# Second MoE of a fused attention and two-MoE kernel: operands in halves, result additions on GpSimd

## The chip, the cores and the metric

One core of one Trainium2 chip. The metric is the device time in microseconds of one execution, the median of three runs. TensorE (PE in the profile) multiplies, VectorE (DVE), ScalarE (ACT) and GpSimd (POOL) work elementwise, and SyncE (SP) issues the transfers. Each engine works through its own instructions in the order in which they are written; semaphores make it wait for others.

## The reference

An attention over 4 batches, 8 heads, 576 positions and 64 columns (half the heads with a local mask, half with a strided one) gives 2304 tokens of 512 columns. Two MoE blocks follow:

```python
gate = 1.0 / (1.0 + np.exp(-(x @ w_gate)));  x = gate * (x @ w_val) @ w_out
h = x @ w_in                                   # 512 -> 2048
g = np.maximum(h, 0.0) + np.log1p(np.exp(-np.abs(h)))
return g @ w_out                               # 2048 -> 512
```

The change lies in the second block (the last three lines).

## The kernel before, in words

Every number is kept as a high and a low part (`xh`, `xl`; `gh`, `gl`), and every product is three matmuls: high by high, high by low, low by high (`mm3`, lines 72 to 74). An operand is made of a float32 tile in two steps: `high` copies it on ScalarE into the rounded part, and `low` subtracts that part from the tile on VectorE or GpSimd (`make`, line 516, with `minus`, line 330). A tile here is 128 partitions by 2 rows of 512 columns, the two rows being the two chunks (`c` or `k`) of the 256 columns of the hidden layer in one group.

The second block (`moe2`, lines 409 to 771) handles the tokens in two halves of 1024 (the last 256 tokens go along with the second half in `short_up` and `short_unit`). Each half goes through 8 groups, so `nn` runs from 0 to 15; `m` counts pairs of groups. Both multiplications are done by a scheme with seven products in place of eight on two-by-two blocks: sums of blocks are formed first, the products are made, and sums of products give the result.

A group `nn` on the way up has seven products, `mul(0)` to `mul(6)`, each six matmuls (`product`). Behind each, `fill(k)` puts some units of the way down (`downs`, numbers in `counts`). A unit is six matmuls into one of three PSUM tiles `ps_y`, and then one VectorE instruction (line 469, or 467 for the first) adds them to a sum in SBUF and so frees the PSUM tile. Between products and units stand hooks: `at(n, k, ph, fn)` registers work for group `n` behind `mul(k)` (`ph` 0) or behind `fill(k)` (`ph` 1). This order, written out by hand, is the order on every engine.

A group gives a 2 by 2 block of activations: `bi` and `bj` with two rows each. `chain` is three ScalarE instructions (absolute value, exponential, logarithm), `finish` one VectorE instruction that adds the positive part. Row 0 of `bi` is done behind `mul(3)`, row 1 of `bj` behind `mul(4)` (`finish(s5)`, line 747), row 0 of `bj` behind `mul(5)` (`add_to(u2)`, chain, and `finish(u2)`, line 752), and row 1 of `bi` behind `mul(6)` (chain, and a `finish` that stands at the head of the next group's first hooks). `snap`, at `mul(0)` of the next group, copies a product into the PSUM tile `ps_b` (line 720) on which `mul(2)` goes on adding.

From the four blocks of a pair of groups (`n1` odd, `n2` after it) seven operands are made: B11, T1, B22, T3, T2, T4, B21. Their tiles `gh` and `gl` come from a pool with three of each: a new operand gets a tile whose units are over. GpSimd makes the sums of blocks in place (`sub(POOL, ...)`): `b12` becomes `b22 - b12`, from which T3 is made, and `b11` becomes `b22 - b11`, from which T2 is made. In the last pair of each half (`m` 3) four plain operands `gj0`, `gi0`, `gj1`, `gi1` replace the seven, and their units add to the results themselves. Shortly before, seven additions of 128x1024 make the results of the sums kept so far (lines 607 to 614, `nl` being 6 and 14). Their tiles `a` and `p6` are called `raw` in the trace, the others `acc`.

The places that are named in the sections below, by the order of the units: the units of T1 stand in `fill(6)` of `n1` and `fill(0)` of `n2`, those of B22 in `fill(1)` and `fill(2)` of `n2`, those of T2 in `fill(5)` and `fill(6)`; in group 7 the first unit of `gj0` stands in `fill(3)`, in group 15 as well. Group 15 has two or three units in each fill. Behind group 15 the last ten units follow, two by two, with hooks between (lines 762 to 770).

Of the kernel before, what the change touches and what calls it, by code (L numbers as in the profile page):

```python
# [40 lines left out]
GC = 2  # L41
# [7 lines left out]
def tile_sparse_attention_moe_moe2(  # L49
# [282 lines left out]
    def high(op, src):  # L332
        nc.scalar.activation(out=op[0], in_=src, func=AF.Copy)  # L333

    def low(op, src, eng):
        minus(eng, op[1], src, op[0].bitcast(F32))
# [58 lines left out]
    def moe2(pools, buf):  # L395
# [55 lines left out]
            load_down(0, home)  # L451


        def unit(key, e, op, y, init, last=False, store=None):
            def go():
                w = at_w[key][0]
                ps = bank(pools, "y", "ps_y")
                o = slice(e * P, (e + 1) * P)
                for c in range(GC):
                    mm3(  # L460
                        ps, (w[:, c, 0, o], w[:, c, 1, o]), tuple(x[:, c, :] for x in op()),
                        c == 0, c == GC - 1,
                    )
                if last:
                    free(key)
                if init:
                    nc.vector.tensor_copy(y, ps)
                else:
                    nc.vector.tensor_tensor(out=y, in0=ps, in1=y, op=ALU.add)  # L469
                if store is not None:  # L470
                    nc.sync.dma_start(out=store, in_=y)

            return go
# [32 lines left out]
        def at(n, k, ph, fn):  # L506
            hooks.setdefault((n, k, ph), []).append(fn)

        def new_op():
            return tuple(  # L510
                pools["g"].tile([P, GC, TB], F32R, tag=x, name=x) for x in ("gh", "gl")
            )
# [3 lines left out]
        def make(op, src, eng, first, second):  # L516
            def begin():
                op.extend(new_op())
                high(op, src)

            at(*first, begin)
            at(*second, lambda: low(op, src, eng))

        def sub(eng, out, a, b):
            return lambda: minus(eng, out, a, b)

        def plus(eng, out, a):
            return lambda: eng.tensor_tensor(out=out, in0=out, in1=a, op=ALU.add)
# [4 lines left out]
        for half in range(2):  # L533
            ac = accs[half]
            for m in range(NM):
                n0 = half * NG2 + 2 * m
                n1, n2, n3 = n0 + 1, n0 + 2, n0 + 3
                b11, b12 = even[m % 2]
                b21, b22 = odd
                key = lambda name: (half, m, name)  # L540
                ops = {x: [] for x in ("B11", "T1", "B21", "B22", "T2", "T3", "T4")}
                get = lambda x, ops=ops: (lambda: ops[x])
                queues.setdefault(n1, [])
                queues.setdefault(n2, [])
                queues.setdefault(n3, [])
                if m == NM - 1:
                    gj0, gi0, gj1, gi1 = [], [], [], []
                    make(gj0, b12, DVE, (n0, 6, 1), (n1, 0, 0))
                    make(gi0, b11, DVE, (n1, 2, 0), (n1, 2, 1))
                    make(gj1, b22, DVE, (n1, 6, 1), (n2, 0, 0))  # L550
                    make(gi1, b21, DVE, (n2, 0, 1), (n2, 1, 0))
                    for nn, par, gj, gi in ((n1, 0, gj0, gi0), (n2, 1, gj1, gi1)):
                        names = (("A11", "A21"), ("A12", "A22"))[par]
                        for t, op, cs in (
                            (2 * half + 1, gj, ("C12", "C22")), (2 * half, gi, ("C11", "C21"))
                        ):
                            for d, c in enumerate(cs):
                                for e in range(2):
                                    d0 = (2 * d + e) * P
                                    t0 = blocks[t][0]  # L560
                                    queues[nn].append(unit(
                                        key(names[d]), e, lambda op=op: op, ac[c][:, e, :], False,
                                        op is gi and e == 1 and (half == 0 or False),
                                        out[d0:d0 + P, t0:t0 + TB] if par else None,
                                    ))
                        if half == 1:
                            for d in range(2):
                                queues[nn].append(short_unit(
                                    key(names[d]), 2 * m + par, d, (2 * m + par) % 2, True
                                ))  # L570
                    continue
                make(ops["B11"], b11, DVE, (n1, 0, 1), (n1, 1, 0))
                at(n1, 1, 1, sub(POOL, b11, b12, b11))
                make(ops["T1"], b11, POOL, (n1, 3, 0), (n1, 3, 1))
                make(ops["B22"], b22, DVE, (n1, 6, 1), (n2, 0, 0))
                at(n1, 6, 1, sub(POOL, b12, b22, b12))
                at(n2, 0, 1, sub(POOL, b11, b22, b11))
                make(ops["T3"], b12, DVE, (n2, 1, 0), (n2, 1, 1))
                make(ops["T2"], b11, DVE, (n2, 2, 0), (n2, 2, 1))
                at(n2, 2, 1, sub(POOL, b11, b21, b11))  # L580
                make(ops["T4"], b11, POOL, (n2, 4, 0), (n2, 4, 1))
                make(ops["B21"], b21, POOL, (n2, 5, 1), (n2, 6, 0))

                def both(nn, name, x, last=True):
                    for e in range(2):
                        queues[nn].append(unit(
                            key(name), e, get(x), ac[target[name]][:, e, :], m == 0,
                            last and e == 1,
                        ))

                alone = half == 0
                both(n1, "A11", "B11", alone)
                if half == 1:
                    for d, name in enumerate(("A11", "A21")):
                        queues[n1].append(short_unit(key(name), 2 * m, d, 0, True))
                both(n1, "S1", "T1")
                for name, x in (("S4", "B22"), ("S3", "T3"), ("S2", "T2")):
                    both(n2, name, x)
                both(n2, "A22", "T4", alone)
                if half == 1:  # L600
                    queues[n2].append(short_unit(key("A22"), 2 * m + 1, 1, 1, True))
                both(n2, "A12", "B21", alone)
                if half == 1:
                    queues[n2].append(short_unit(key("A12"), 2 * m + 1, 0, 1, True))


            nl = half * NG2 + NG2 - 2
            at(nl, 1, 1, plus(POOL, ac["C11"], ac["a"]))
            at(nl, 3, 1, plus(POOL, ac["C12"], ac["C22"]))
            at(nl, 6, 1, plus(DVE, ac["a"], ac["p6"]))  # L610
            at(nl + 1, 0, 0, plus(DVE, ac["C12"], ac["a"]))
            at(nl + 1, 0, 1, plus(POOL, ac["a"], ac["p7"]))
            at(nl + 1, 1, 0, plus(POOL, ac["C22"], ac["a"]))
            at(nl + 1, 1, 1, plus(POOL, ac["C21"], ac["a"]))
# [37 lines left out]
        def chain(src, dst):  # L652
            nc.scalar.activation(out=dst, in_=src, func=AF.Abs)
            nc.scalar.activation(out=dst, in_=dst, func=AF.Exp, scale=-1.0)
            nc.scalar.activation(out=dst, in_=dst, func=AF.Ln, bias=1.0)

        def finish(src, dst):
            nc.vector.scalar_tensor_tensor(
                out=dst, in0=src, scalar=0.0, in1=dst, op0=ALU.max, op1=ALU.add
            )  # L660
# [31 lines left out]
        for nn in range(N):  # L692
# [13 lines left out]
            def mul(k, ps, a, b, first, stop, then_do=None):  # L706
                product(ps, a, x[b], first, stop)
                if then_do:
                    then_do()
                if not last and (half == 0 or a not in OPS[:3]):  # L710
                    fetch(goes, then, a)
                run_hooks(k, 0)
# [24 lines left out]
            if half == 1 and not last:  # L737
# [5 lines left out]
            add_to(s5, Bk, s5)  # L743
            chain(s5, bj[:, 1, :])
            fill(4)
            mul(5, D, "S4", "B22", False, True)
            finish(s5, bj[:, 1, :])
            add_to(u2, D, u2)
            chain(u2, bj[:, 0, :])
            fill(5)  # L750
            mul(6, Bk, "A22", "T4", False, True)
            finish(u2, bj[:, 0, :])
            chain(Bk, bi[:, 1, :])
            hooks.setdefault((nn + 1, 0, 0), []).insert(
                0, lambda Bk=Bk, d=bi[:, 1, :]: finish(Bk, d)
            )
# [680 lines left out]
```

## Time and profile before

| | us |
|---|---|
| runs (3), median and extremes | 901.35 (899.46 to 901.43) |
| the profiled execution | 902.33 |
| its span (first to last instruction) | 900.5 |
| PE busy in the span | 874.0 (97%) |
| DVE, ACT, POOL busy | 608.5, 413.6, 453.6 |
| mean granted TensorE clock | 0.988 |

The span is the time between the first and the last instruction of the profiled execution. An engine is busy while it executes; instructions of TensorE overlap, and a matmul of 512 columns lasts longer than the distance between two of them. "Idle before" counts from the end of the instruction before it on the same engine, and the name behind it is what ended the wait.

### The profile page before, as it was taken

How to read it: one execution, taken by the hardware profiler on the slowest of the kernel's cores; microseconds unless marked ns; L12 is line 12 of the kernel's file. 1: busy time of each engine (PE TensorE's matmuls, PEld its weight loads, DVE VectorE, ACT ScalarE, POOL GpSimd, SP SyncE). 2: the span in 40 equal slices, each digit the busy share in tenths (PEclk: the TensorE clock that was granted, in tenths of full speed). 3: DMA queues.
4: the chain of work that ended last, by engine and by line, in shares of the span. 5: the costliest groups of instructions: out<-in, count | busy, mean ns of one | idle time of the engine just before them, and what ended most of it. 6: DMA issues, size and time to landing. Idle time of an engine off the chain costs nothing.

```text
span 900.5 us, 15316 instructions
## 1 busy us (share of the span) xinstructions
PE 874.0 (97%) x6022; PEld 729.4 (81%) x6022; DVE 608.5 (68%) x893; ACT 413.6 (46%) x663; POOL 453.6 (50%) x353
## 2 busy tenths in 40 slices
PE   7699999999999999999999999999999999999997
PEld 5578878888888888888888887888778888888786
DVE  6596776278878887788884545565786464657755
ACT  2366544333333232333243556667557565555541
POOL 5373421047796786687677425655642243343510
PEclk9699999999999999999999999999999999999999
DMA  9686450034764575566552435655455664545403
GB/s 272 175 240 166 121 157 1 1 117 138 253 229 175 187 256 168 182 230 209 195 210 94 141 98 190 199 199 191 153 199 186 204 192 153 176 148 171 137 1 116
DMA packets 59974, 149.33 MB, mean 166 GB/s; under 512 B 6048, under 2 KB 6560, under 8 KB 59904
## 3 DMA queue, kind: packets, MB, share of 16 engines
q1 hardware_dynamic: 59616, 147.75, 50.9%
q8 instruction: 47, 0.77, 0.4%
q10 hardware_dynamic: 288, 0.62, 0.2%
q14 instruction: 23, 0.19, 0.1%
HBM read 112.17 MB, written 36.18 MB: 165 GB/s over the span
## 4 chain that ended last, share of the span: by engine, by line
PE 66%; DVE 7%; ACT 3%; POOL 2%; issue 2%; DVEq 0%; POOLq 0%; ACTq 0%
PE ps_y L73 9%; PE ps_y L72 9%; PE ps_y L74 9%; PE ps_v L74 4%; PE ps_v L72 4%; PE ps_v L73 4%; PE ps_g L72 4%; PE ps_g L73 4%; PE ps_g L74 4%; PE ps_h L74 3%; PE ps_h L73 3%; PE ps_h L72 3%; PE ps_b L73 2%; PE ps_b L72 2%; PE ps_b L74 2%
## 5 line engine op out<-in xcount | busy, mean ns | idle before, releaser
L330 POOL TENSOR_TENSOR b<-b,b 128x1024 f32<-128x1024 f32 x24 | 60.3, 2524 | 110.3 <-DVE gl L330 60.9
L241 ACT ACTIVATE gh<-ps_v 128x512 fp32r<-128x512 f32 (+1 forms) x60 | 33.2, 554 | 128.8 <-DVE ps_v L284 128.8
L304 DVE TENSOR_TENSOR acc<-ps_y,acc 128x512 f32<-128x512 f32 (+1 forms) x100 | 61.9, 632 | 39.0 <-PE ps_y L74 38.3
L469 DVE TENSOR_TENSOR acc<-ps_y,acc 128x512 f32<-128x512 f32 x72 | 48.7, 687 | 43.4 <-PE ps_y L74 43.3
L189 POOL TENSOR_TENSOR a<-f,e 128x512 f32<-128x512 f32 x32 | 41.4, 1294 | 58.3 <-DVE e L139 57.9
L242 DVE TENSOR_TENSOR gl<-ps_v,gh 128x512 fp32r<-128x512 f32 (+1 forms) x60 | 38.3, 638 | 40.0 <-ACT gh L241 40.0
L330 POOL TENSOR_TENSOR gl<-b,gh 128x1024 fp32r<-128x1024 f32 x18 | 43.3, 2406 | 37.6 <-ACT gh L333 37.6
L284 DVE TENSOR_TENSOR ps_v<-ps_v,sg 128x512 f32<-128x512 f32 (+1 forms) x60 | 38.5, 642 | 28.0 <-PE ps_v L74 26.6
L333 ACT ACTIVATE gh<-b 128x1024 fp32r<-128x1024 f32 x50 | 52.5, 1050 | 10.3 <-POOL b L330 9.7
L73 PE MATMUL ps_y<-gl,w12h 128*128 128x512 f32 (+1 forms) x148 | 55.3, 374 | 1.0 <-DVE gl L330 1.0
L72 PE MATMUL ps_y<-gh,w12h 128*128 128x512 f32 (+1 forms) x148 | 55.9, 378 | 0.5 <-ACT gh L333 0.4
L72 PE MATMUL ps_y<-gh,w02h 128*128 128x512 f32 (+1 forms) x144 | 54.8, 381 | 0.8 <-ACT acc L302 0.5
L73 PE MATMUL ps_y<-gl,w02h 128*128 128x512 f32 (+1 forms) x144 | 54.0, 375 | 0.4 <-DVE gl L242 0.4
L330 DVE TENSOR_TENSOR gl<-b,gh 128x1024 fp32r<-128x1024 f32 x32 | 47.6, 1486 | 8.9 <-ACT gh L333 8.9
L126 DVE SCALAR_TENSOR_TENSOR f<-raw,ps_x 128x512 uint32<-128x512 uint32 x68 | 46.8, 688 | 9.8 <-POOL w11l L153 2.1
L74 PE MATMUL ps_y<-gh,w02l 128*128 128x512 f32 (+1 forms) x140 | 52.3, 373 | 0.4 <-POOL w02l L153 0.4
L74 PE MATMUL ps_y<-gh,w12l 128*128 128x512 f32 (+1 forms) x140 | 52.2, 373 | 0.2 <-POOL w12l L153 0.2
L177 POOL TENSOR_TENSOR pair<-a,pair 128x512 fp32r<-128x512 f32 x32 | 41.4, 1295 | 18.9 <-ACT pair L176 18.2
L139 DVE SCALAR_TENSOR_TENSOR e<-raw,ps_x 128x512 f32<-128x512 uint32 x68 | 46.7, 687 | 2.3
L132 DVE TENSOR_SCALAR ps_x<-f 128x512 uint32<-128x512 uint32 x68 | 46.8, 688 | 1.1
L122 DVE TENSOR_SCALAR ps_x<-raw 128x512 uint32<-128x512 uint32 x68 | 46.5, 684 | 0.0
L72 PE MATMUL ps_g<-xh,w00h 128*128 128x512 f32 (+1 forms) x120 | 45.3, 378 | 0.0
(341 smaller groups left out, 2768.8 us busy)
## 6 DMA issues: line engine op xcount, KB each, us to landing
raw<-in_w_dram SPq DMA_DIRECT2D x68, 512.0 KB, 3.9
in_s<-pair SPq DMA_DIRECT2D x32, 512.0 KB, 2.8
xh<-in_s SPq DMA_DIRECT2D x64, 256.0 KB, 3.3
out_s<-pair SPq DMA_DIRECT2D x28, 512.0 KB, 2.7
xl<-in_s SPq DMA_DIRECT2D x56, 256.0 KB, 3.5
out_dram<-acc SPq DMA_DIRECT2D x16, 256.0 KB, 2.0
w10h<-out_s SPq DMA_DIRECT2D x6, 512.0 KB, 5.9
w10l<-out_s SPq DMA_DIRECT2D x6, 512.0 KB, 4.1
```

What stands on the lines that cost most here:

```text
L72: nc.tensor.matmul(ps, lhsT=lh, rhs=rh, start=first, stop=False, **kw)
L73: nc.tensor.matmul(ps, lhsT=lh, rhs=rl, start=False, stop=False, **kw)
L74: nc.tensor.matmul(ps, lhsT=ll, rhs=rh, start=False, stop=last, **kw)
L122: nc.vector.tensor_scalar(out=part, in0=high, scalar1=3, scalar2=0x3FFFFFFF, op0=ALU.logical_shift_left, op1=ALU.bitwise_and,)
L126: nc.vector.scalar_tensor_tensor(out=f, in0=high, scalar=0xC0000000, in1=part, op0=ALU.bitwise_and, op1=ALU.bitwise_or,)
L132: nc.vector.tensor_scalar(out=e, in0=f, scalar1=0xFF800000, scalar2=None, op0=ALU.bitwise_and)
L139: nc.vector.scalar_tensor_tensor(out=e.bitcast(F32), in0=low, scalar=2.0 ** -52, in1=x.bitcast(F32), op0=ALU.mult, op1=ALU.mult,)
L177: nc.gpsimd.tensor_tensor(out=l, in0=src, in1=h.bitcast(F32), op=ALU.subtract)
L304: nc.vector.tensor_tensor(out=y, in0=ps[:, 0:n], in1=y, op=ALU.add)
L330: eng.tensor_tensor(out=out, in0=a, in1=b, op=ALU.subtract)
L333: nc.scalar.activation(out=op[0], in_=src, func=AF.Copy)
L469: nc.vector.tensor_tensor(out=y, in0=ps, in1=y, op=ALU.add)
```

## The change

The operands that are made last in a group (B22 of each pair, and `gj0`, `gj1`, `gi1` of the last pair of each half) are made row by row, each row 512 columns, the row that is done first ahead of the other (`make_late`). A unit takes its two chunks in the order `order`: chunk 1 first, except for units of `gi`. The two GpSimd sums that read `b22` (for T3 and T2) are cut into rows as well. `finish(s5)` and `finish(u2)` are written ahead of the transfer and the hooks of their product, and a hook of phase 0.5 stands behind the last chain of a group. Two of the seven result additions of each half go from VectorE to GpSimd.

```diff
-        def unit(key, e, op, y, init, last=False, store=None):
+        def unit(key, e, op, y, init, last=False, store=None, order=(1, 0)):
...
-                for c in range(GC):
+                for i, c in enumerate(order):
                     mm3(
                         ps, (w[:, c, 0, o], w[:, c, 1, o]), tuple(x[:, c, :] for x in op()),
-                        c == 0, c == GC - 1,
+                        i == 0, i == GC - 1,
                     )
...
+        def make_late(op, src, nn, k, times):
+            row = lambda k: tuple(x[:, k, :] for x in op)
+
+            def begin():
+                op.extend(new_op())
+                high(row(k), src[:, k, :])
+
+            other = 1 - k
+            for when, fn in zip(times, (
+                begin, lambda: low(row(k), src[:, k, :], DVE),
+                lambda: high(row(other), src[:, other, :]),
+                lambda: low(row(other), src[:, other, :], DVE),
+            )):
+                at(nn + when[0] // 7, when[0] % 7, when[1], fn)
+
+        LATE_J = (1, ((5, 0), (5, 1), (6, 0), (6, 0.5)))
+        LATE_I = (0, ((5, 1), (6, 0.5), (7, 0), (7, 1)))
...
-                    make(gj0, b12, DVE, (n0, 6, 1), (n1, 0, 0))
+                    make_late(gj0, b12, n0, *LATE_J)
                     make(gi0, b11, DVE, (n1, 2, 0), (n1, 2, 1))
-                    make(gj1, b22, DVE, (n1, 6, 1), (n2, 0, 0))
-                    make(gi1, b21, DVE, (n2, 0, 1), (n2, 1, 0))
+                    make_late(gj1, b22, n1, *LATE_J)
+                    make_late(gi1, b21, n1, *LATE_I)
...
+                                        (0, 1) if op is gi else (1, 0),
...
-                make(ops["B22"], b22, DVE, (n1, 6, 1), (n2, 0, 0))
-                at(n1, 6, 1, sub(POOL, b12, b22, b12))
-                at(n2, 0, 1, sub(POOL, b11, b22, b11))
+                make_late(ops["B22"], b22, n1, *LATE_J)
+                for k, when in ((1, (n1, 5, 1)), (0, (n1, 6, 1))):
+                    at(*when, sub(POOL, b12[:, k, :], b22[:, k, :], b12[:, k, :]))
+                for k, when in ((1, (n1, 6, 1)), (0, (n2, 0, 1))):
+                    at(*when, sub(POOL, b11[:, k, :], b22[:, k, :], b11[:, k, :]))
...
-            at(nl, 6, 1, plus(DVE, ac["a"], ac["p6"]))
-            at(nl + 1, 0, 0, plus(DVE, ac["C12"], ac["a"]))
+            at(nl, 6, 1, plus(POOL, ac["a"], ac["p6"]))
+            at(nl + 1, 0, 0, plus(POOL, ac["C12"], ac["a"]))
...
-            mul(5, D, "S4", "B22", False, True)
-            finish(s5, bj[:, 1, :])
+            mul(5, D, "S4", "B22", False, True, lambda d=bj[:, 1, :]: finish(s5, d))
             add_to(u2, D, u2)
             chain(u2, bj[:, 0, :])
             fill(5)
-            mul(6, Bk, "A22", "T4", False, True)
-            finish(u2, bj[:, 0, :])
+            mul(6, Bk, "A22", "T4", False, True, lambda d=bj[:, 0, :]: finish(u2, d))
             chain(Bk, bi[:, 1, :])
+            run_hooks(6, 0.5)
```

## Rows read from the trace of the kernel before

**Rows 1.** Windows: us, busy of PE, PEld, DVE, ACT, POOL (x instructions), PEclk, DMA, GB/s.

```profile
512.30:901.00 388.70, 376.34 (x1828) 315.50 (x1826) 235.91 (x298) 222.97 (x337) 153.75 (x66) 0.99 0.50 161
635.50:639.30 3.80, 3.80 (x11) 2.93 (x11) 3.80 (x4) 0.00 (x0) 1.67 (x1) 0.55 0.00 1
863.20:875.40 12.20, 12.20 (x55) 10.10 (x55) 7.72 (x12) 3.79 (x6) 0.00 (x0) 1.00 0.01 1
```

**Rows 2.** Timeline of PE, matmuls that waited: start, us, instruction, [idle before <-releaser].

```profile
548.95 0.50 PE L73 MATMUL ps_y<-gl,w10l 128*128 128x512 f32 x1 [0.16 <-POOL gl L330]
...
554.86 0.50 PE L72 MATMUL ps_y<-gh,w12h 128*128 128x512 f32 x1 [0.40 <-ACT gh L333]
...
556.38 0.50 PE L73 MATMUL ps_y<-gl,w12h 128*128 128x512 f32 x1 [1.02 <-DVE gl L330]
...
634.98 0.50 PE L73 MATMUL ps_y<-gl,w10h 128*128 128x512 f32 x1 [2.08 <-DVE gl L330]
...
657.22 0.50 PE L72 MATMUL ps_b<-w01h,xl 128*128 128x512 f32 x1 [0.15 <-ACT ps_b L720]
...
661.01 0.50 PE L72 MATMUL ps_y<-gh,w10h 128*128 128x512 f32 x1 [0.78 <-DVE acc L469]
...
776.70 0.50 PE L73 MATMUL ps_y<-gl,w01l 128*128 128x512 f32 x1 [0.26 <-DVE gl L330]
...
853.50 0.47 PE L72 MATMUL ps_y<-gh,w01l 128*128 128x512 f32 x1 [1.67 <-issue]
...
886.22 0.50 PE L72 MATMUL ps_y<-gh,w02l 128*128 128x512 f32 x1 [0.72 <-DVE acc L469]
...
889.41 0.50 PE L72 MATMUL ps_y<-gh,w02h 128*128 128x512 f32 x1 [0.15 <-DVE acc L469]
```

**Rows 3.** Instructions writing ps_y after 512 us: ns min/median/max, first and last start.

```profile
L73 PE MATMUL ps_y<-gl,w10h x24: 389/390/537, 543.2 to 662.0; 128*128 128x512 f32 x24
```

**Rows 4.** Lines L330, L308, L687, then groups of ACT: lengths in ns.

```profile
L330 DVE TENSOR_TENSOR gl<-b,gh x32: 1207/1218/3072, 537.3 to 884.3; 128x1024 fp32r<-128x1024 f32 x32
...
L330 DVE TENSOR_TENSOR xh<-sg,xh x4: 679/682/693, 704.3 to 852.1; 128x512 fp32r<-128x512 f32 x4
...
L308 POOL TENSOR_TENSOR xl<-acc,xh x14: 737/1292/1632, 471.5 to 545.8; 128x512 fp32r<-128x512 f32 x10, 128x256 fp32r<-128x256 f32 x4
...
L687 ACT ACTIVATE xh<-sg x4: 614/624/633, 703.6 to 849.4; 128x512 fp32r<-128x512 f32 x4
...
L333 ACT ACTIVATE gh<-b 128x1024 fp32r<-128x1024 f32 x50 | 52.5, 1050 | 10.3 <-POOL b L330 9.7 <-DVE b L658 0.5
```

**Rows 5.** Timeline of POOL and DVE around 845 us.

```profile
845.24 2.41 POOL L330 TENSOR_TENSOR gl<-b,gh 128x1024 fp32r<-128x1024 f32 x1 [4.21 <-ACT gh L333]
...
845.80 2.94 DVE L528 TENSOR_TENSOR raw<-raw 128x1024 f32<-128x1024 f32 x1
...
852.12 0.68 DVE L330 TENSOR_TENSOR xh<-sg,xh 128x512 fp32r<-128x512 f32 x1
```

**Rows 6.** Timeline of DVE and ACT, groups 1 to 2.

```profile
552.07 0.69 DVE L658 SCALAR_TENSOR_TENSOR b<-raw,b 128x512 f32<-128x512 f32 x1 [1.43 <-ACT b L655]
...
551.95 0.58 ACT L653 ACTIVATE b<-ps_b 128x512 f32<-128x512 f32 x1
...
554.71 0.58 ACT L720 ACTIVATE ps_b<-ps_h 128x512 f32<-128x512 f32 x1
```

**Rows 7.** Timeline of DVE and ACT, groups 5 to 7.

```profile
632.04 2.88 DVE L330 TENSOR_TENSOR gl<-b,gh 128x1024 fp32r<-128x1024 f32 x1 [0.26 <-ACT gh L333]
...
648.07 2.30 DVE L658 SCALAR_TENSOR_TENSOR b<-raw,b 128x512 f32<-128x512 f32 x1 [0.56 <-ACT b L655]
...
654.40 3.08 DVE L528 TENSOR_TENSOR raw<-raw 128x1024 f32<-128x1024 f32 x1
...
656.59 0.58 ACT L720 ACTIVATE ps_b<-ps_h 128x512 f32<-128x512 f32 x1
```

**Rows 8.** Timeline of DVE behind the last group.

```profile
884.34 1.23 DVE L330 TENSOR_TENSOR gl<-b,gh 128x1024 fp32r<-128x1024 f32 x1 [3.37 <-ACT gh L333]
```

## The prediction

> **What bounds the kernel now.** The busy shares by window come first: in the second MoE TensorE is busy 376.3 of 388.7 us [rows 1], so only the gaps between matmuls can be won; the matmuls themselves stay the same. The timeline of PE then shows where it waited [rows 2]. To price a wait I need the even pace: 55 matmuls in 12.20 us without a gap [rows 1], or 0.23 us from start to start. A matmul lasts 0.39 us [rows 3], so it overlaps the next by 0.16; one that waited lasts 0.50 [rows 2], 0.11 more. A wait thus costs its idle time plus 0.16 plus 0.11, or idle plus 0.27.
>
> By place [rows 2]: (a) 548.95, the low part of T1, 0.43. (b) 554.86 and 556.38, operand B22 of group 2, 0.67 and 1.29. (c) 634.98, B22 of group 6, 2.35; right behind it the granted clock averages 0.55 for 3.8 us [rows 1], half speed most of that time, after TensorE had been idle 2.08 us. That costs 0.45 x 3.8 = 1.7, so (c) is 4.05. (d) 657.22, the snapshot in group 7, 0.42. (e) 661.01, a unit waiting for VectorE to free its tile, 1.05. (g) 776.70, B22 again, 0.53; group 14 has a second one alike. (i) 853.50 in group 15, 1.94: its releaser reads "issue", but the unit needs a tile that VectorE frees late. (j) 886.22 and 889.41 behind the last group, 0.99 and 0.42. Without (a), which the change doesn't touch, 1.96 + 4.05 + 0.42 + 1.05 + 1.06 + 1.94 + 1.41 = **11.9 us** can be won.
>
> Why they are late is told by the lengths. A low part of 128x1024 on VectorE takes 1.22 us, but 3.07 at worst; 128x512 takes 0.68 [rows 4]. The cause is seen around 845 us: GpSimd runs 845.24 to 847.65, VectorE starts at 845.80 and ends at 848.74, 1.09 us after GpSimd [rows 5]. A VectorE instruction with both inputs in SBUF stands until GpSimd's is over.
>
> **The halves.** Twelve operands are cut: three B22, `gj0`, `gj1` and `gi1` in each half of the tokens. Each costs two ScalarE halves of 0.62 for one of 1.05 and two VectorE halves of 0.68 for one of 1.22 [rows 4]: 0.2 and 0.14 more, which lie beside TensorE's work. Twelve GpSimd sums become 24 of 1.29 [rows 4] for 12 of 2.41; GpSimd is busy 154 of 389 us [rows 1], so what counts is that one half holds VectorE for 1.29 at most. No transfer is added, and SP's queue keeps its order; `finish` ahead of a transfer's issue is on another engine. The early half's ScalarE part falls into the time in which VectorE does `add_to(u2)`, so the next chain isn't put off.
>
> The late half starts after `finish(u2)`, ahead of the last chain: 0.62 on ScalarE and 0.68 on VectorE, plus at most 1.29 of standing, 2.6 us together. In group 1 `finish(u2)` ends at 552.76 [rows 6], so the late half is there by 555.4, and only the fifth matmul of the unit needs it, 0.9 us into a unit that is due at 554.5. (b) goes as a wait for the operand.
>
> But a new wait stands behind it. The last chain now starts at 552.76 + 0.62 = 553.4 in place of 551.95; from its start to that of the snapshot it was 2.76 us, 1.05 of them the whole high part [rows 6, 4], which leaves 1.8 (the two overlap a little), so the snapshot runs 555.2 to 555.8, and `mul(2)` is due around 555.7. I leave 0.5 of (b): **1.5 won**. Queued behind the late half on VectorE are the addition of `fill(6)` and `finish(Bk)`; three PSUM tiles give that addition 2.7 us.
>
> (c): the low part starts at 632.04 [rows 7], after a chain of 1.9 and a high part of 1.05, so ScalarE was free for the late half at 629.1; by 631.7 it is done, before the unit wants it at 632.9. **4.05 won**, clock included.
>
> (g): group 12 and 14 have more units between, and the snapshot's slack is over 3 us there; **1.1 won**.
>
> (d) and (e): in group 6 the chain is bound by the other engines. `finish(s5)` takes 2.30 at 648.07, held by GpSimd's low part of T4, and the snapshot begins at 656.59 [rows 7]. With 4.05 us gone TensorE is that much ahead, and the others only in part: GpSimd's addition into C11 now meets the low part of T3, which stands for it, and T2, T4 and both chains follow. I estimate 1.0 us more of lateness against TensorE, plus 0.4 for the late half's wait for `finish(u2)`, less 0.43 for a half in place of a whole high part: (d) grows from 0.42 to 1.4. (e) goes, as the 3.08 us addition [rows 7] leaves VectorE. **0.1 won**.
>
> **The additions.** Four leave VectorE, two in each half of the tokens; they took 3.08 and 2.94 [rows 7, 5], and about 1.2 each for the other two, 8.4 together. On GpSimd they are four of 2.41. Undisturbed, one takes 2.41 there against 1.22 [rows 5, 4], so GpSimd has up to 4 x 1.2 = 4.8 us more to do than VectorE would at its best; at the two places that matter VectorE took more than GpSimd does. The Trainium skill speaks against such a move (GPSIMD Engine Reference, 3.1 Elementwise: elementwise work stays on VectorE as a rule, a large add being 1.96 times as long on GpSimd). The trace agrees on the ratio, 2.41 to 1.22, but not at these two places, 2.41 to 3.08 and 2.94; by the rule alone the sum would be 4.8 us smaller, by the rows it is as below. Queued behind the moved ones on GpSimd are the three additions that were there. In group 7 the chain of five starts around 655 and `C12` is ready after two, near 660; its first unit ends near 661.
>
> (i): here three things stand. The pool has three tiles of each kind; the early operand `gj0` now takes the one that B21 took, so B21's high part must wait for the last S2 unit. VectorE's addition of 845.80 [rows 5] needs that unit's eviction of 0.69, so the unit ends near 845.0; B21's high part, 1.05, now starts there in place of 844.1, and GpSimd's low part of 2.41 runs from 846.1 to 848.5. `gj0`'s late half behind it on VectorE stands until then and ends at 849.1. Then the moved addition starts on GpSimd as soon as the last S2 unit is added, at 849.7, holds the port to 852.1, and the short operand's low part (852.12 to 852.80 before [rows 5]) stands to 852.7. The eviction behind it comes at 853.3, as late as now. **0.2 won** of 1.94.
>
> (j): the last high part of `gi1` waits for the short chain; with halves its low part takes 0.68 at 884.0 in place of 1.23 from 884.34 [rows 8]. (886.22) goes, 0.4 is left one unit later. **1.0 won**.
>
> Sum: 1.5 + 4.05 + 1.1 + 0.1 + 0.2 + 1.0 = 7.95. The profiled execution took 902.33, 0.98 above the median of 901.35; 902.33 - 7.95 = 894.4, and against the median **893.4**.
>
> **The rivals.** *All goes* (0.17): the new waits at (b), (d), (i) and (j) stay hidden, 901.35 - 11.9 = 889.4. For it: my new waits hang on tenths. Against: GpSimd's hold is seen in every row that is late.
>
> *GpSimd's sums are late* (0.08): VectorE's first addition into `C12` stands for GpSimd, and every eviction with it. Price: GpSimd's 4.8 us more in full, 893.4 + 4.8 = 898.2. It decides once GpSimd's second sum ends after the first unit of `gj0`, a margin of about 1 us in group 7 and 7 in group 15. (It is the case of the Trainium skill's rule above.)
>
> *The snapshot takes over* (0.11): the last chain starts 1.3 us later (0.69 of `finish(u2)` and 0.62), and 1.6 more where GpSimd holds `finish(u2)` as it held the one at 648.07 (2.30 for 0.69 [rows 7]). Against the slack from the snapshot's end to `mul(2)`, read along the timeline of ACT and PE (0.4, 2.4, 1.4 us in groups 2, 4, 6; none in 7; 1.9 in 8; over 3 later) 2.9 us leaves 2.5 + 0.5 + 1.5 + 3.0 + 1.0 = 8.5; with 2.1 left at (i) and (j) that is 10.6 of 11.9: 900.0, no change.
>
> *VectorE's queue stands* (0.09), on the other side: the late half's low part is now ahead of the addition of `fill(6)`. VectorE stands 0.65 for ScalarE and 1.29 for GpSimd, in groups 6 and 14 2.41 for it. If those evictions were the last word each time, eight places of 1.94 and two of 3.06 make 21.6: 901.35 - 11.9 + 21.6 = 911.1. It decides where an eviction comes more than two units, 2.7 us, late. Against it: only (e), (i) and (j) wait for an eviction today.
>
> **How the numbers follow.** The forecast has 0.55. Below 0.3% (2.7 us) a measurement of this kernel can't be told from no change. The forecast, all goes and late sums are faster: 0.80; the snapshot is the same: 0.11; the queue is slower: 0.09. The range leaves out the last two and reaches from all goes, with 0.4 for the spread of the runs, to late sums with 0.8: 889.0 to 899.0.
>
> **What would show it.** Right: no PE wait for `gl` by VectorE in groups 2, 6, 12 and 14; no fall of the clock after group 6; additions of 128x1024 on VectorE gone from line 528; the first matmul of `mul(2)` in group 7 waiting over 1 us for line 720; a wait near (i) still over 1 us; (a) unchanged. Wrong: a wait over 2 us anywhere, above all in group 7, which could bring the low clock back; VectorE additions into `acc` that wait for line 528; or new waits in groups 4, 8 and 10.

## The result and the profile after

The kernel after took **890.39 us** (median of 4 runs, 889.45 to 891.42) beside 901.39 (899.46 to 902.29) for the kernel before: a ratio of 0.9881, with a 95% interval of 0.9861 to 0.9902. The forecast was 893.4, in a range of 889.0 to 899.0. Later runs of both, on another chip, gave 891.27 (6 runs) beside 898.99 (11 runs), 0.9907 (0.9887 to 0.9927). So the gain is 8 to 11 us, and the first question is what part of it belongs to the change.

The page of the kernel after, head and part 1 (busy us, share, instructions):

```profile
span 889.4 us, 15355 instructions
...
PE 867.6 (98%) x6022; PEld 726.4 (82%) x6022; DVE 598.9 (67%) x901; ACT 416.5 (47%) x675; POOL 464.8 (52%) x369
```

The profiled execution took 891.42 us. VectorE lost 9.6 us of work and GpSimd gained 11.2, while TensorE executes the same 6022 matmuls. Where the second MoE begins is told by the instructions that write `ps_h` (ns min/median/max, first to last start). First the kernel before, then the kernel after:

```profile
L72 PE MATMUL ps_h<-xh x112: 277/390/397, 512.8 to 878.7; 128*128 128x512 f32 x96, 128*128 128x256 f32 x16
```

```profile
L72 PE MATMUL ps_h<-xh x112: 277/389/396, 510.2 to 868.5; 128*128 128x512 f32 x96, 128*128 128x256 f32 x16
```

The kernel after is 2.6 us ahead before anything that was changed has run. From this matmul to the end of the span I call the **stretch**: 900.5 - 512.8 = 387.7 us before, 889.4 - 510.2 = 379.2 after. The change won 8.5 us in its own place; the forecast for that was 7.95. The other 2.6 us came from the start of the program, and the experiments return to them. All experiments are measured by their stretch, since it leaves the start out.

The windows of the kernel after (columns as in [rows 1]), and on the timeline of PE every wait that is left in the stretch:

```profile
510.20:889.40 379.20, 372.41 (x1825) 314.17 (x1823) 226.08 (x305) 225.68 (x349) 164.67 (x82) 1.00 0.51 164
```

```profile
546.36 0.50 PE L73 MATMUL ps_y<-gl,w10l 128*128 128x512 f32 x1 [0.17 <-POOL gl L330]
...
553.20 0.50 PE L72 MATMUL ps_b<-w01h,xl 128*128 128x512 f32 x1
...
649.31 0.50 PE L72 MATMUL ps_b<-w01h,xl 128*128 128x512 f32 x1 [0.60 <-ACT ps_b L741]
...
698.09 0.50 PE L73 MATMUL ps_y<-gl,w00h 128*128 128x512 f32 x1 [0.36 <-DVE gl L330]
...
843.30 0.47 PE L72 MATMUL ps_y<-gh,w01l 128*128 128x512 f32 x1 [1.59 <-issue]
...
878.23 0.50 PE L72 MATMUL ps_y<-gh,w02h 128*128 128x512 f32 x1 [0.17 <-DVE acc L469]
```

Six waits are left where [rows 2] has ten: at idle plus 0.27 each, 0.44, some 0.2 (the length of 0.50 and the later starts alone betray it), 0.87, 0.63, 1.86 and 0.44. The one at 698.09 waits for B11 of group 8, was there before as well (0.35 idle at 707.05), and the prediction didn't list it. With this one and the second of (g) the kernel before has twelve waits, 12.95 us with the low clock behind (c); the six after make 4.44. The difference is 8.5, the gain of the stretch, so the price of idle plus 0.27 for a wait holds here. No VectorE low part of B22 is waited for any more, and the mean granted clock of the stretch is 1.00.

The biggest wait left is (i). The timelines of ACT, POOL and DVE ahead of it, in the kernel after:

```profile
834.88 1.58 ACT L333 ACTIVATE gh<-b 128x1024 fp32r<-128x1024 f32 x2 [0.79 <-PE ps_y L74]
```

```profile
836.02 2.41 POOL L330 TENSOR_TENSOR gl<-b,gh 128x1024 fp32r<-128x1024 f32 x1 [5.31 <-ACT gh L333]
839.65 2.40 POOL L546 TENSOR_TENSOR raw<-raw 128x1024 f32<-128x1024 f32 x1 [1.23 <-DVE raw L469]
```

```profile
836.49 2.48 DVE L330 TENSOR_TENSOR gl<-b,gh 128x512 fp32r<-128x512 f32 x1 [1.68 <-ACT gh L333]
838.89 0.68 DVE L469 TENSOR_TENSOR raw<-ps_y,raw 128x512 f32<-128x512 f32 x1
...
840.86 1.73 DVE L330 TENSOR_TENSOR xh<-sg,xh 128x512 fp32r<-128x512 f32 x1
842.52 1.27 DVE L469 TENSOR_TENSOR acc<-ps_y,acc 128x512 f32<-128x512 f32 x2
```

B21's high part waits 0.79 for its tile, GpSimd makes the low part from 836.02 to 838.43, and the late half on VectorE stands until 838.97, 2.48 us for an instruction of 0.68. The moved addition runs on GpSimd from 839.65 to 842.05, the short operand's low part stands beside it for 1.73 us, and only then comes the eviction (842.52) that frees the tile. That eviction and the next, which read PSUM, take 1.27 together, no more than elsewhere.

### The profile page after: what moved, and what is told of

Its sections match the earlier page's. It is cut to its first block, busy times and chain, and to the rows that moved or that the text cites. A ratio compares the mean times of both kernels' runs of the same rounds, so it can differ in the third digit from the quotient of the medians.

```text
span 889.4 us, 15355 instructions
## 1 busy us (share of the span) xinstructions
PE 867.6 (98%) x6022; PEld 726.4 (82%) x6022; DVE 598.9 (67%) x901; ACT 416.5 (47%) x675; POOL 464.8 (52%) x369
## 4 chain that ended last, share of the span: by engine, by line
PE 68%; DVE 5%; ACT 3%; POOL 2%; issue 2%; DVEq 0%; POOLq 0%; ACTq 0%
PE ps_y L72 10%; PE ps_y L73 10%; PE ps_y L74 10%; PE ps_v L74 4%; PE ps_v L73 4%; PE ps_v L72 4%; PE ps_g L74 4%; PE ps_g L73 4%; PE ps_g L72 4%; PE ps_h L72 3%; PE ps_h L73 3%; PE ps_h L74 3%; PE ps_b L72 2%; PE ps_b L73 2%; PE ps_b L74 2%
## 5 line engine op out<-in xcount | busy, mean ns | idle before, releaser
L330 POOL TENSOR_TENSOR b<-b,b 128x512 f32<-128x512 f32 (+1 forms) x36 | 62.1, 1739 | 102.2 <-DVE gl L330 59.4
L333 ACT ACTIVATE gh<-b 128x1024 fp32r<-128x1024 f32 (+1 forms) x62 | 54.9, 888 | 36.7 <-DVE b L679 25.2
L330 POOL TENSOR_TENSOR gl<-b,gh 128x1024 fp32r<-128x1024 f32 x18 | 43.3, 2408 | 39.4 <-ACT gh L333 39.4
L330 DVE TENSOR_TENSOR gl<-b,gh 128x512 fp32r<-128x512 f32 (+1 forms) x44 | 50.0, 1140 | 16.1 <-ACT gh L333 16.0
L72 PE MATMUL ps_v<-xh,w01h 128*128 128x512 f32 (+1 forms) x120 | 44.8, 374 | 0.0
```

Of the source, the lines that this page charges most:

```text
L72: nc.tensor.matmul(ps, lhsT=lh, rhs=rh, start=first, stop=False, **kw)
L330: eng.tensor_tensor(out=out, in0=a, in1=b, op=ALU.subtract)
```

## The experiments

Twelve runs, all on the same stretch. "Low clock" is time in the stretch at the lower of TensorE's two levels (1.2 in place of 2.4 GHz), ahead of the last 5 us.

| run | what differs | stretch | low clock | median or single time |
|---|---|---|---|---|
| before | | 387.7 | 3.4 | 901.39 (4 runs) |
| e10 | before, once more | 386.9 | none | 901.91 (1) |
| e2 | before + additions | 389.7 | 6.8 | 900.98 (10) |
| e3 | before + sums | 385.0 | none | 897.64 (1) |
| e9 | before + sums + additions | 385.5 | none | 898.17 (1) |
| e1 | after - additions | 385.2 | 6.8 | 896.39 (5) |
| e4 | after - sums cut | 380.7 | none | 895.49 (1) |
| e12 | after - one addition | 386.1 | 6.8 | 899.02 (1) |
| after, e8 | | 379.2, 379.2 | none | 890.39 (4), 891.27 (6) |
| e5 | after, late half first | 379.2 | none | 892.49 (1) |
| e6 | after + B21 by rows | 377.4 | none | 891.08 (1) |
| e7 | after + all of GpSimd by rows | 376.2 | none | 887.99 (6) |
| e11 | e7 + B11 of group 8 by rows | 375.7 | none | 889.12 (1) |

**The halves without the moved additions** (e1), from the kernel after:

```diff
-            at(nl, 6, 1, plus(POOL, ac["a"], ac["p6"]))
-            at(nl + 1, 0, 0, plus(POOL, ac["C12"], ac["a"]))
+            at(nl, 6, 1, plus(DVE, ac["a"], ac["p6"]))
+            at(nl + 1, 0, 0, plus(DVE, ac["C12"], ac["a"]))
```

> The changed kernel with its two moved additions per half of the tokens back on VectorE. I compare the stretch from the first matmul of the second MoE to the end of the span: 387.7 us before (900.5 - 512.8), 379.2 after (889.4 - 510.2). My theory (operands were late, and that is what the halves cure): the waits for B22 in groups 2, 6, 12 and 14, the low clock behind group 6, and most of the tail stay gone, but in groups 7 and 15 the 1.2 us additions stand again ahead of the evictions on VectorE: about 1.5 us more in each, 382.2, between 381 and 383.5; the median near 893.4. Rival (relieving VectorE of the additions is the gain): 385 or more, median 897 or more.

385.2 us and a median of 896.39, ratio 0.9957 (0.994 to 0.9975): 6.0 us more than the kernel after. On VectorE's timeline in group 15, then on PE's in groups 7 and 15, then in the window behind the second wait:

```profile
840.56 1.23 DVE L546 TENSOR_TENSOR raw<-raw 128x1024 f32<-128x1024 f32 x1
...
842.90 1.22 DVE L546 TENSOR_TENSOR acc<-acc,raw 128x1024 f32<-128x1024 f32 x1
844.04 0.69 DVE L330 TENSOR_TENSOR xh<-sg,xh 128x512 fp32r<-128x512 f32 x1
844.64 1.28 DVE L469 TENSOR_TENSOR acc<-ps_y,acc 128x512 f32<-128x512 f32 x2
```

```profile
652.98 0.50 PE L72 MATMUL ps_y<-gh,w10h 128*128 128x512 f32 x1 [1.46 <-DVE acc L469]
...
845.43 0.77 PE L72 MATMUL ps_y<-gh,w01l 128*128 128x512 f32 x1 [2.83 <-issue]
```

```profile
844.50:851.40 6.90, 5.97 (x14) 4.75 (x15) 2.71 (x5) 0.48 (x1) 6.82 (x3) 0.51 0.00 0
```

The additions now run undisturbed, 1.23 and 1.22, and are still too long: both lie in VectorE's queue ahead of the low part and the eviction that TensorE needs. That costs 1.46 + 0.27 = 1.73 in group 7 and 1.24 in group 15; and behind the longer wait the clock was granted at 0.51, which costs 0.49 x 5.97 = 2.9. Together 5.9 of the 6.0. My expectation was missed: 385.2 lies above its range, where the rival had put the run. Without the clock, which it left out, the run would be near 382.3.

**The additions without the halves** (e2), the same two lines changed in the kernel before.

> The kernel before with only the two additions per half of the tokens moved to GpSimd. My theory: all waits for B22 stay, with the low clock; in group 7 some 0.7 us of the wait for an eviction goes; in group 15 the moved addition holds the port ahead of VectorE's low part and then of the short operand's, and the wait there grows from 1.7 to about 2.9 us. Stretch 388.2, between 387.2 and 388.7; no change in the median. Rival (relieving VectorE is the gain): 382 or less, median 895 or less.

389.7 us, and a ratio of 1.0013 (0.9994 to 1.0032): nothing won. On VectorE's timeline in group 15, on GpSimd's, on PE's, and in the window behind its wait:

```profile
845.13 3.13 DVE L330 TENSOR_TENSOR gl<-b,gh 128x1024 fp32r<-128x1024 f32 x1 [0.26 <-ACT gh L333]
848.18 2.85 DVE L330 TENSOR_TENSOR xh<-sg,xh 128x512 fp32r<-128x512 f32 x1
```

```profile
844.78 2.40 POOL L528 TENSOR_TENSOR raw<-raw 128x1024 f32<-128x1024 f32 x1
847.26 3.23 POOL L528 TENSOR_TENSOR acc<-acc,raw 128x1024 f32<-128x1024 f32 x1
```

```profile
851.73 0.77 PE L72 MATMUL ps_y<-gh,w01l 128*128 128x512 f32 x1 [2.74 <-issue]
```

```profile
851.30:854.70 3.40, 2.97 (x7) 2.42 (x8) 1.53 (x3) 0.00 (x0) 3.32 (x2) 0.50 0.00 0
```

With `gj0` whole, its low part meets the two additions on GpSimd and each holds up the other: 3.13 for VectorE's 1.22, 3.23 for GpSimd's 2.41, then 2.85 for a 0.68. VectorE is spared two additions of 1.2 to 2.9 us and pays 1.9 and 2.2 in standing; the wait grew from 1.67 to 2.74 and the clock fell behind it (1.5 us), which puts the run above my range of 387.2 to 388.7.

**The sums in rows, alone** (e3), in the kernel before:

```diff
-                at(n1, 6, 1, sub(POOL, b12, b22, b12))
-                at(n2, 0, 1, sub(POOL, b11, b22, b11))
+                for k in (1, 0):
+                    at(n1, 6, 1, sub(POOL, b12[:, k, :], b22[:, k, :], b12[:, k, :]))
+                for k in (1, 0):
+                    at(n2, 0, 1, sub(POOL, b11[:, k, :], b22[:, k, :], b11[:, k, :]))
```

> The kernel before with only GpSimd's sums for T3 and T2 cut into rows, in their old places. My theory (VectorE's low part stands for the whole GpSimd instruction that runs when it arrives): in groups 12 and 14 the wait for B22 goes, in group 6 it shrinks from 2.1 to about 1.1 us idle and the clock doesn't fall, in group 2 it stays; stretch 384.0, between 383 and 385.5. Rival (operands are late only because they are begun late): 387.7, within 0.4.

385.0 us, as expected. B22 is still late in groups 2 and 6, in group 6 by 1.14 in place of 2.08, and the waits of groups 12 and 14 are gone:

```profile
554.62 0.50 PE L73 MATMUL ps_y<-gl,w12h 128*128 128x512 f32 x1 [1.16 <-DVE gl L330]
...
632.39 0.50 PE L73 MATMUL ps_y<-gl,w10h 128*128 128x512 f32 x1 [1.14 <-DVE gl L330]
```

**The kernel after with these sums whole** (e4), at `(n1, 6, 1)` and `(n2, 0, 1)`, their old places:

> The changed kernel with GpSimd's sums for T3 and T2 whole, at the old places. My theory: the late half of B22 stands up to 1.1 us longer; that shows in group 2, 0.6 us of waiting, and through the later chain by about 0.5 us in group 7; stretch 380.4, between 379.6 and 381. Rival (the cut sums are what brings the gain): 383 or more.

380.7 us, in the range that was expected. Two waits come back, one each in groups 2 and 6, seen on PE's timeline of e4, then on VectorE's:

```profile
555.90 0.50 PE L73 MATMUL ps_y<-gl,w12h 128*128 128x512 f32 x1 [0.49 <-DVE gl L330]
...
637.58 0.50 PE L73 MATMUL ps_y<-gl,w10l 128*128 128x512 f32 x1 [0.47 <-DVE gl L330]
```

```profile
553.51 2.33 DVE L330 TENSOR_TENSOR gl<-b,gh 128x512 fp32r<-128x512 f32 x1 [0.70 <-ACT gh L333]
...
634.71 2.82 DVE L330 TENSOR_TENSOR gl<-b,gh 128x1024 fp32r<-128x1024 f32 x1
```

The first wait is for B22, whose late half takes 2.33 beside a whole sum (1.22 beside a row in the kernel after). The second is not for B22: the low part behind it has 1024 columns and is that of T3. VectorE's late half of B22 ahead of it takes 2.25 (628.58) in place of 1.14, so T3's low part starts 2.0 us ahead of its unit in place of 3.0, and takes 2.8 in both kernels. I had expected 0.5 us of waiting in group 7 in its place; the wait for the snapshot there grew by 0.2. So the cut sums are worth 1.9 to 2.7 us in the kernel before, and 1.5 in the kernel after together with the earlier places of their rows.

**Sums and additions without the halves** (e9), both edits in the kernel before.

> The kernel before with the sums in halves at their old places and the two additions on GpSimd, the operands whole: the change without its halves. From the first ps_h matmul of the second MoE to the end of the span, where before has 387.7 us, sums alone 385.0 and the kernel after 379.2. Theory: the halves carry what is left. B22 stays late in groups 2 and 6 as with the sums alone (2.1 and 1.4), gj0's whole low part and the short operand's stand beside the moved additions in group 15 as with the additions alone (2.9 and some low clock), and the last two waits stay (1.3): 386.3 us (385.0 to 388.0). Rival: the halves only lengthen the work, as their order already proved idle, and shorter sums with free VectorE do it all: 381.5 us or less.

385.5 us, nearer to the theory than to its rival, and below its 386.3 because the clock did not fall this time. On PE's timeline B22 is late again in group 2, and group 15 has its long wait:

```profile
554.58 0.50 PE L73 MATMUL ps_y<-gl,w12h 128*128 128x512 f32 x1 [1.16 <-DVE gl L330]
...
849.32 0.47 PE L72 MATMUL ps_y<-gh,w01l 128*128 128x512 f32 x1 [2.73 <-issue]
```

The halves, with the earlier `finish` and the earlier places of the sums, are worth 385.5 - 379.2 = 6.3 us there; the additions, on top of the halves, 6.0 (3.1 without the clock); and the additions without the halves less than nothing (e3 to e9, 0.5 lost: the wait for an eviction in group 7 falls from 0.78 to 0.23, that of group 15 grows from 1.67 to 2.73). The halves without the additions win nothing either (e3 to e1, 385.0 to 385.2), but there a fall of the clock (2.9) takes the 2.7 that they would win. So the full gain needs both.

**One addition only** (e12), the second one back on VectorE:

```diff
-            at(nl + 1, 0, 0, plus(POOL, ac["C12"], ac["a"]))
+            at(nl + 1, 0, 0, plus(DVE, ac["C12"], ac["a"]))
```

> The kernel after with the second of the two additions (C12 += a) back on VectorE, the first (a += p6) on GpSimd. It stands between the kernel after (379.2 us) and the one with both on VectorE (385.2, of which 2.8 is low clock). Theory: VectorE takes its instructions in order, so the second addition waits there for GpSimd's first (2.41 us) and everything behind it too: in group 15 the short operand's low part starts after that addition, 1.4 us later than in the kernel after, and in group 7 the eviction into acc ends near 654.4, 3 us late. 383.7 us, up to 386.5 if TensorE's clock falls behind such a wait: no better than with both on VectorE. Rival: what counts is VectorE's work, 1.2 us of it back in each half: about 382 us or less, between the two.

386.1 us, within the theory's bounds and 0.9 worse than with both on VectorE (0.4 without the clock, which fell behind both waits here, 0.5 x 3.40 each). Without the clock it would be near 382.7, close to what the rival named; it is the waits that decide against the rival, 2.13 and 2.90 us where e1 has 1.46 and 2.83. VectorE's timeline in group 7, PE's in both groups, and the windows behind the waits:

```profile
653.27 1.22 DVE L546 TENSOR_TENSOR acc<-acc,raw 128x1024 f32<-128x1024 f32 x1 [1.91 <-POOL raw L546]
654.42 0.68 DVE L469 TENSOR_TENSOR acc<-ps_y,acc 128x512 f32<-128x512 f32 x1
```

```profile
655.16 0.76 PE L72 MATMUL ps_y<-gh,w10h 128*128 128x512 f32 x1 [2.13 <-DVE acc L469]
...
849.29 0.47 PE L72 MATMUL ps_y<-gh,w01l 128*128 128x512 f32 x1 [2.90 <-issue]
```

```profile
655.20:658.60 3.40, 3.40 (x8) 2.73 (x9) 1.61 (x3) 0.00 (x0) 3.32 (x2) 0.50 0.95 295
849.80:853.20 3.40, 3.40 (x9) 2.63 (x8) 1.27 (x2) 0.00 (x0) 3.32 (x2) 0.50 0.00 0
```

VectorE waits 1.91 us for GpSimd's first addition, and every eviction stands behind it. It is no matter of VectorE's amount of work: with half of the work moved the waits are longer than with none.

**The late half first** (e5): every unit takes chunk 0 ahead of chunk 1, also where chunk 1 is made first.

```diff
-        def unit(key, e, op, y, init, last=False, store=None, order=(1, 0)):
+        def unit(key, e, op, y, init, last=False, store=None, order=(0, 1)):
...
-                                        (0, 1) if op is gi else (1, 0),
+                                        (0, 1),
```

> The kernel after, but every unit of the second MoE multiplies the columns that are made last first. Measured from the first ps_h matmul of the second MoE to the end of the span, where the kernel after has 379.2 us. Theory: the gain comes from the shorter instructions and the earlier start, as the late half is there before its unit starts (by 1.5 us in group 6); only in group 2, where it ends 0.4 us after the unit's first matmul, is something lost: 379.6 us (379.2 to 380.2). Rival: the units run on the early half while the late one is made; then groups 2, 6, 12 and 14 each wait for gl by VectorE again, 0.5 or more each: 381.5 us or more.

379.2 us, no loss at all (the units of `gi` take chunk 0 first as in the kernel after). In group 2 the unit now waits some 0.2 us for its late half:

```profile
553.14 0.50 PE L73 MATMUL ps_y<-gl,w12h 128*128 128x512 f32 x1
```

In exchange the 0.2 that the snapshot cost right behind it in the kernel after is gone. So the order in which a unit reads its halves wins nothing here. What is left for the halves to win by is that each instruction is short and starts as early as its own row; this is told by exclusion, as no run has the earlier `finish` without the halves.

**GpSimd's long holds by rows** (e6: B21's low part and the addition of `p6`; e7: those of T1 and T4 as well). `make` gets a switch `rows`, which these three operands set, and the addition is cut by a helper like it:

```diff
-            at(*second, lambda: low(op, src, eng))
+            def end():
+                if eng is not nc.gpsimd or not rows:
+                    return low(op, src, eng)
+                for k in (1, 0):
+                    low(tuple(x[:, k, :] for x in op), src[:, k, :], eng)
+
+            at(*second, end)
```

> The kernel after, with GpSimd's low part of B21 in two rows of 128x512 and its addition of p6 in two rows. Theory: the wait in group 15 (1.83 us) stands for GpSimd's long holds alone: the late half's low part takes 1.2 to 1.4 us in place of 2.48, the short operand's low part under 1.3 in place of 1.73, and most of the wait goes: 377.5 us (377.0 to 378.2). Rival: it is the wait of B21's high part for its tile (0.79 us at 834.88) that sets the time there: 378.6 us or more, with over 1 us left at that unit.

> As the run before, and GpSimd's low parts of T1 and T4 in two rows too. Theory: the waits for GpSimd's T1 (0.43), for the snapshot of group 7 (0.87, late since a chain's end stood 2.29 us beside T4) and of group 15 (1.83) go: 376.1 us (375.6 to 377.0), a median near 887.3 us. Rival: the rows make GpSimd itself later (0.18 us more for each operand) and what VectorE wins is lost behind GpSimd: 377.4 us or more, no better than the run before.

377.4 and 376.2 us, both as expected. VectorE's timeline of e6 ahead of the place of (i):

```profile
837.90 1.36 DVE L330 TENSOR_TENSOR gl<-b,gh 128x512 fp32r<-128x512 f32 x1 [1.67 <-ACT gh L333]
...
841.16 1.06 DVE L330 TENSOR_TENSOR xh<-sg,xh 128x512 fp32r<-128x512 f32 x1
```

These were 2.48 and 1.73, and the wait is gone. B21's tile wait is still 0.79 in e6, so it doesn't set the time by itself; giving it a fourth tile was not tried. In e7 the median is 887.99 (0.9874 of before, 0.9853 to 0.9894), beside 891.27 for the kernel after on the same chip: 3.3 us by medians, 3.0 by stretch. It is the fastest kernel with more than one run. **B11 of group 8 by rows** (e11), on ScalarE and VectorE, on top of it; `make` then cuts both steps:

```diff
-                make(ops["B11"], b11, DVE, (n1, 0, 1), (n1, 1, 0))
+                make(ops["B11"], b11, DVE, (n1, 0, 1), (n1, 1, 0), half == 1 and m == 0)
```

> All rows of GpSimd as in the fastest kernel so far (376.2 us), and B11 of group 8 in two rows on ScalarE and VectorE. Theory: its low part is ready 0.4 us ahead of the matmul that now waits 0.63: 375.5 us (375.4 to 375.8). Rival: the second ScalarE half puts the next snapshot off by 0.2 us and the wait moves there: 376.0 us or more.

375.7 us: the wait is gone and 0.5 of 0.63 won. Its single time, 889.12, says nothing against that, since its second MoE began at 511.7 and that of e7 at 510.1.

**Both kernels once more** (e8, e10).

> The kernel after once more. If the 2.6 us by which its first execution was ahead of the kernel before at the start of the second MoE is a matter of the execution, its stretch is 379.2 us again (379.0 to 379.5), while the start of the second MoE lies anywhere between 509 and 513 us, as in the six executions so far. Rival: the change itself moved the start: 510.2 again, within 0.3.

> The kernel before once more. If its second MoE repeats as that of the kernel after did (379.2 twice), the stretch is 387.7 us (387.3 to 388.1) with the wait of group 6 and the low clock behind it, and only the start differs (509 to 513). Rival: the low clock behind group 6 comes in some executions alone; then 386.0 us.

The kernel after repeats its stretch, 379.2, from a start at 509.1 us; the kernel before begins at 513.2 and takes 386.9. Here the rival was right that the low clock comes only in some executions, but not on the size, and 386.9 lies below my range. On PE's timeline of e10, and in the window behind the first wait:

```profile
635.43 0.50 PE L73 MATMUL ps_y<-gl,w10h 128*128 128x512 f32 x1 [2.09 <-DVE gl L330]
...
656.80 0.50 PE L72 MATMUL ps_b<-w01h,xl 128*128 128x512 f32 x1 [0.88 <-ACT ps_b L720]
```

```profile
635.50:639.30 3.80, 3.80 (x17) 3.13 (x18) 3.80 (x4) 1.02 (x2) 2.15 (x1) 1.00 0.06 18
```

The wait is the one of [rows 2], 2.09 for 2.08, but the clock stayed at 1.00 where [rows 1] has 0.55; TensorE came to the snapshot of group 7 sooner and waited 0.88 there in place of 0.15. Half of the low clock was hidden by that later wait. Against this execution the change wins 386.9 - 379.2 = 7.7 us, against the first one 8.5; the forecast of 7.95 lies between.

## Why the prediction was right, point by point

- **(b), 1.5 of 1.96.** 0.2 is left where I left 0.5, and it is the wait that I named, for the snapshot. That the unit needs its late half only from the fifth matmul on saved nothing, as e5 shows. VectorE's late half stood beside GpSimd's sum and took 1.22 (550.87 to 552.09), within the bound of 0.68 plus 1.29.
- **(c), 4.05.** All of it went, the clock with it. The term has two parts of different kind: 2.35 was in both profiled executions of the kernel before, while 1.7 of low clock was in one of them, and in the other (e10) half of it came back as (d). That I could count it was luck of the execution that I read.
- **(d) and (e), 0.1.** (d) grew, as forecast, but to 0.87 in place of 1.4; (e) went. The mechanism was `finish(s5)`, which still stood 2.29 us beside GpSimd's low part of T4; in e7, where that low part is in rows, it took 1.19 and (d) is gone. The size was my estimate of lateness, 0.5 too much, and the sign that I had named, over 1 us of waiting there, did not come (0.60). VectorE in the kernel after, then in e7:

```profile
640.60 2.29 DVE L679 SCALAR_TENSOR_TENSOR b<-raw,b 128x512 f32<-128x512 f32 x1 [1.44 <-ACT b L676]
```

```profile
640.48 1.19 DVE L693 SCALAR_TENSOR_TENSOR b<-raw,b 128x512 f32<-128x512 f32 x1 [1.67 <-ACT b L690]
```

- **(g), 1.1.** Gone, and with the sums alone too.
- **(i), 0.2.** The walk held to 0.2 us. Put 10.2 us earlier, as (i) itself is (so the last time agrees by this choice, the steps before it do not), its forecast is: high part at 834.8, GpSimd 835.9 to 838.3, late half's end 838.9, the addition 839.5 to 841.9, the eviction at 843.1. Measured: 834.88, 836.02 to 838.43, 838.97, 839.65 to 842.05, 843.20. 1.86 of 1.94 is left.
- **(j), 1.0.** 0.44 is left of 1.41; shown by e2 and e3, which keep both waits, and by e1, which has one.

The stretch gave 0.6 more than the sum: (b) 0.3 and (d) 0.5 better, (i) and (j) a little worse. The median is 3.0 below the forecast, 2.4 more than the stretch explains. In the two profiled executions the rest is the start: I took 902.33 for a property of the kernel, but that execution began its second MoE 2.6 us later than the one of the kernel after, and the start was no part of my working. For the other runs the start was not read; that it makes up the difference of the medians too is not shown, though the later medians, 7.7 apart, lie on the other side of 8.5.

The rivals. *All goes* failed: at (b), (d), (i) and (j) a wait stayed. *GpSimd's sums are late* did not happen: one eviction waited 1.03 for a sum of GpSimd (660.90), which I had named as a sign of being wrong, but no matmul waited for it. The rule of the Trainium skill behind it (GPSIMD Engine Reference, 3.1 Elementwise, elementwise work on VectorE as a rule) agrees with e2 and e9, where the move won nothing, and not with e1 beside after, where it is worth 6.0 us. Durations alone do not tell it: what counted here was VectorE's queue ahead of one eviction in group 7 and one in group 15. *VectorE's queue stands* did not happen in the kernel after; evictions that come late behind a standing VectorE are what e12 shows, though there VectorE stands for a moved addition and not for a late half. *The snapshot takes over* came true for 1.1 us out of its 8.5.

One step was wrong though the sum came out. I priced the additions by their durations at two places, 3.08 and 2.94 against 2.41, and held the halves to win nearly everything else. By that the kernel after with its additions back on VectorE would lose little more than a wait like (e), 1.05. It lost 6.0 (385.2, e1): 1.73 in group 7, 1.24 more in group 15, and 2.9 of low clock. That the full sum came out owes something to both parts being in the kernel.

## What to carry to other kernels

Where VectorE and GpSimd work on the same memory, cut first the long GpSimd instructions that stand beside a VectorE instruction which someone waits for: a pair of rows costs GpSimd 0.2 us undisturbed and 0.6 where VectorE comes in between (3.00 for 2.41 in e6 and e7), and cutting three low parts and one addition won 3.0 us here without moving anything. Before a step is moved to another engine, ask what is queued behind each of its consumers; a chain moved by half puts a wait for the other engine into an in-order queue, and here the waits were longer than with nothing moved (e12 beside e1). Compare two profiles from the first changed instruction on, and not by their whole spans.

## What the hardware showed that was not expected

**The start.** In the profiled executions of kernels that share all instructions ahead of the second MoE, it began between 509.1 (e8) and 513.2 us (e10). The low clock at the start differs as well; these windows are the first 60 us of before and of after:

```profile
0.00:60.00 60.00, 47.60 (x1045) 37.19 (x1048) 40.67 (x75) 23.58 (x42) 29.70 (x51) 0.86 0.79 226
```

```profile
0.00:60.00 60.00, 47.62 (x1091) 37.14 (x1095) 43.14 (x79) 25.42 (x45) 29.84 (x52) 0.94 0.85 239
```

0.86 against 0.94 over 60 us would be 4.8 us of full clock, enough for those 2.6, with 46 matmuls more done by then in the kernel after. But e1 began earlier still, at 509.4, with 13.7 us of low clock in it, and e7 at 510.1 with 20.5, more than any other; so the clock isn't the whole of it. The difference arises early: TensorE's 1500th matmul starts at 88.1 us before and at 85.5 after, 2.6 apart already. What else differs stays open.

**The clock behind a wait.** In these runs TensorE was idle for 2.08 to 2.90 us eight times in the stretch, and the granted clock fell to its lower level behind six of them: 2.08 (before), 2.10 and 2.74 (e2), 2.83 (e1), 2.13 and 2.90 (e12). It stayed up behind 2.09 (e10) and 2.73 (e9), and behind the 1.59 of the kernel after and the 1.67 of e10. Such a wait therefore has two prices, its own and up to 2.9 us more, and one profile shows only one of them.

**Standing goes both ways.** One of GpSimd's additions took 3.2 us between two VectorE instructions in e2. The Trainium skill says of the port that both use (SBUF — State Buffer, Who interferes with whom) that whoever issues first gets it for the whole instruction, and the other blocks. The rows agree: GpSimd's second addition, 847.26 to 850.49, is 0.8 us longer than the first and stands until VectorE's low part ends at 848.26; VectorE's next one then stands until 850.49. Evictions from PSUM beside GpSimd's additions kept their 0.68 (654.42 in e12, two together 1.28 in e1 and 1.27 in the kernel after).
